# Top-32 attention and a low-rank mixer on one core: another mask for the first batch's heads, a parameter's scaling on GpSimd, and seven buffers for the rounds' maxima

## The chip, the core and the metric

The kernel runs on one core of a Trainium2 chip. A core has a matrix engine (TensorE, PE in the profile), a vector engine (VectorE, DVE), a scalar engine (ScalarE, ACT), a general engine (GpSimd, POOL) and a queue engine (SyncE, SP). Each engine works through its own list of instructions in order, and waits on semaphores where an instruction needs another engine's result. The metric is the time of one execution on the device in microseconds. The kernel before took 1663.71 us in the median of three runs (1663.66 to 1663.92).

## What is computed

Eight batches of eight attention heads, 576 rows each, keep only the 32 largest scores of every row. A mixer with a low-rank matrix over the rows and a two-layer network over the channels follows.

```python
scores = scale * np.matmul(q, k.transpose(0, 1, 3, 2))        # (8, 8, 576, 576), head_dim 64
kth = np.partition(scores, -32, axis=-1)[..., -32:-31]
scores = np.where(scores >= kth, scores, -1e9)
attn = softmax(scores)
x = np.matmul(attn, v) -> (8, 576, 512)
u = x + ((x.T @ U) @ V).T                                      # per batch, rank 32
out = u + np.maximum(u @ w_ch1, 0.0) @ w_ch2                   # 512 -> 2048 -> 512
```

The four parameters of the mixer (U, V, w_ch1, w_ch2) reach the kernel as float64 numbers, that is as pairs of 32-bit words; the kernel turns them into float32 itself.

## The kernel before

**Steps.** Two heads make a pair, so a batch has four pairs (`NPAIR`) and the kernel 32. A step is a tile of 128 rows of a pair, for both heads: t = 0 to 3; the last 64 rows of both heads share one tile, t = 4. In the first batch (pairs 0 to 3) each tile is a step of its own, 20 steps in all (lines 1200 to 1269). In the later batches t = 3 and t = 4 make one step. This document calls the two heads of a step its lanes; lane 1 comes first in every loop, then lane 0.

**The search for the 32 largest.** `front` (line 454) is a generator, advanced piece by piece. In each lane VectorE takes the eight largest of a row (line 507, `first`), strikes them out (line 520, MATCH_VALUE_LOAD and MATCH_REPLACE8) and takes the next eight (line 525), three rounds in all; the eighth value of the last round is the threshold. The rounds' maxima lie in `m8`, allocated anew in each round from a ring of four buffers (line 522). In the first batch the rows are 576 wide; from the second batch on VectorE works on folded rows of 304.

**The masks.** `ways` (line 441) says how each lane is masked once the threshold is known. In the first batch lane 1 of a full tile is "pooled": GpSimd makes the gap (line 530, a comparison and a multiplication by -3e38) and adds it to the scores (line 531), both issued at the end of the step itself. Lane 0, and the one lane of t = 4, take the "gap" way: at the beginning of the next step ScalarE scales the threshold (line 551, `least`), computes the gap with Relu (line 554), and GpSimd subtracts it (line 555). In the later batches both lanes take the "gap" way. The last full tile and the tail of pair 3 have an "early" lane, masked on VectorE. After the mask, `weigh` (line 437) takes the exponential on ScalarE.

**The parameters.** `next_params` (line 218) is called six times per pair in the first batch, besides one call before the loop: after round 1 of t = 0, 1 and 2, and after round 3 of t = 0, 1 and 3. Each call moves three parameters on by a stage: it joins the oldest (`f64_join`: VectorE shifts the bits, line 188; GpSimd adds twice, lines 189 and 191), starts the conversion of the next (`f64_parts`), and loads a third (line 154, on SP's queue, into a ring of three `raw` buffers). The conversion is three ScalarE passes: the scaling (line 176) reads the high words, a second (line 177) rewrites the low words, a third (line 180, Sign) rewrites the high words in place. The passes wait in a list, from which `fill`, called four times a step, takes one each; what is left is issued by the next `next_params`. There are 36 parameters' pieces: 4 of U and V, 16 of w_ch1 and 16 of w_ch2, nearly all 128 x 512 words. A call that finds `len(params)` pieces still unloaded converts piece 35 - `len(params)`.

**Order.** The order on every engine is that of the program (`manual_schedule`); a step of the first batch issues on each engine, in this order: the gap of the step before (lines 551 to 555); the matmuls and the copies of the next step's scores (lines 336, 390 to 392); the values and the transposes of earlier steps (lines 694, 617, 618, 703); `fill`; round 1; `next_params`; `fill`; copies of the next pair's q and k (line 323); round 2; the exponentials of the step before (line 439); `fill`; round 3; `next_params`; the end of the step (lines 530, 531); `fill`.

**The network.** The two layers of a batch are cut into single matmuls, handed out between the steps of the following batch (lines 816 and 834). So the first batch has none of them, and the last batch's come behind the last step (`closing`).

Of the kernel before, what the change touches and what calls it, by code (L numbers as in the profile page):

```python
# [8 lines left out]
F32 = mybir.dt.float32  # L9
U8 = mybir.dt.uint8  # L10
U32 = mybir.dt.uint32
AF = mybir.ActivationFunctionType
ALU = mybir.AluOpType

TOPK = 32
NEG = -3.0e38


RESCALE = 2.0**-112
# [7 lines left out]
def kernel(  # L27
# [28 lines left out]
    nc = tc.nc  # L56
    B, H, S, D = q.shape
    P = 128
# [8 lines left out]
    NPAIR = H // 2  # L67
# [13 lines left out]
    const = ctx.enter_context(tc.tile_pool(name="const", bufs=1))  # L81
    loads = ctx.enter_context(tc.tile_pool(name="loads", bufs=1))
    attn = ctx.enter_context(tc.tile_pool(name="attn", bufs=2))
    small = ctx.enter_context(tc.tile_pool(name="small", bufs=8))
# [37 lines left out]

    nudge = const.tile([P, 1], F32, name="nudge")
    nc.vector.memset(nudge, TINY)
    eps = const.tile([P, 1], F32, name="eps")
    nc.vector.memset(eps, 1e-9)

# [10 lines left out]
        return slice(h * D, (h + 1) * D)  # L138

    SLAB = 512  # L140
    spare = []


# [13 lines left out]
    def f64_parts(raw, out):  # L157

        n, w = raw.shape[0], raw.shape[-1] // 2
        d = "p f" if len(raw.shape) == 3 else "p"
        low, hi = (raw.rearrange(f"{d} (w two) -> {d} w two", two=2)[..., i] for i in range(2))
        low8 = raw.bitcast(U8).rearrange(f"{d} (w eight) -> {d} w eight", eight=8)[..., 3]
        if out is None:
            if not spare:

                uT = mlpp.tile([P, NC, S], F32, tag="uT", name="uT")
                words = uT.rearrange("p c n -> p (c n)").bitcast(U32)  # L170
                spare.extend(words[:, i * SLAB : (i + 1) * SLAB] for i in range(NT))
            out = spare.pop()[0:n, 0:w]
        bits = out.bitcast(U32)
        lows, his = low.bitcast(F32), hi.bitcast(F32)
        passes.extend((
            lambda: nc.scalar.activation(bits.bitcast(F32), his, AF.Copy, scale=RESCALE),
            lambda: nc.scalar.activation(
                lows, low8, AF.Identity, bias=four[0:n], scale=-(1 + 2.0**-10) * 2.0**-26
            ),
            lambda: nc.scalar.activation(his, his, AF.Sign, bias=nudge[0:n]),  # L180
        ))
        return hi, bits, low
# [258 lines left out]
    def ways(g, t):  # L441

        if (g, t) == (NPAIR - 1, NT - 1):
            return (0,), (), (1,)
        if (g, t) == (NPAIR - 1, NT):
            return (0,), (), ()
        if t == NT:
            return (), (), (0,)
        return ((), (1,), (0,)) if g < NPAIR else ((), (), (1, 0))

    def eased(g, t):
        return bool(ways(g, t)[2])

    def front(tiles):

        lanes = []
        for g, t in tiles:  # L460
            if t == 0:
                dens[g] = small.tile([P, 2 * NT + 1], F32, tag="den", name="den", bufs=3)
            S2, den = S2s.pop((g, t)), dens[g]
            early, pooled, gaps = ways(g, t)
            n = S2.shape[1]
            fold_of = folds.pop((g, t), None)
            for c in (1, 0) if n == 2 else (0,):
                slot = c if n == 2 or len(tiles) == 1 else 2
                spot = CH * c + t if g >= NPAIR else 2 * t + c
                lanes.append((  # L470
                    slot,
                    S2[:, c],
                    den[:, spot : spot + 1],
                    [a[:, c] for a in fold_of] if fold_of else None,
                    "early" if c in early else "pooled" if c in pooled else "gap" if c in gaps else "",
                ))
        W = len(lanes)
        first = small.tile([P, 3, 8], F32, tag="first", name="first", bufs=3)
        nmax = small.tile([P, 3], F32, tag="nmax", name="nmax", bufs=4)
        curs, places, ms = {}, {}, {}  # L480
        halves = [(lane[0], *lane[3]) for lane in lanes if lane[3]]
        for at_, step in ((0, 0), (0, 1), (8, 0)):
            for slot, upper, lower in halves:
                spot = upper[:, HALF + at_ : HALF + at_ + 8]
                if step:
                    nc.vector.match_replace(lower, spot, lower, NEG)  # L486
                else:
                    nc.vector.max(spot, lower)  # L488
        for slot, chunk, _, fold_of, _ in lanes:
            if fold_of:  # L490
                curs[slot] = fold_of[0]
            else:
                curs[slot] = chunk
                if slot == 2:
                    places[slot] = attn.tile([P, S], F32, tag="tplace", name="place", bufs=1)
                elif (g, t) == (NPAIR, NT):
                    places[slot] = attn.tile([P, TAIL + S], F32, tag="scale", name="place", bufs=1)[:, 0:S] if slot else (
                        attn.tile([P, NT + 1, P], F32, tag="PTt", name="place", bufs=1)
                    ).rearrange("p c n -> p (c n)")[:, 0:S]
                else:  # L500
                    places[slot] = attn.tile(
                        [P, 2, HALF + TOPK // 2], F32, tag="upper", name="upper"
                    ).rearrange("p c n -> p (c n)")[:, 0:S]
            ms[slot] = first[:, slot]
        order = [lane[0] for lane in lanes]
        for c in order:
            nc.vector.max(ms[c], curs[c])  # L507
        yield
        for i in range(1, TOPK // 8):
            if i == 1:  # L510
                nc.scalar.mul(nmax[:, 0:W], first[:, 0:W, 0], -SCALE)
                Es = {}
                for c, chunk, _, _, way in lanes:
                    if way == "early":
                        Es[c] = attn.tile([P, S], F32, tag="E", name="E")
                        weigh(chunk, Es[c], nmax[:, c : c + 1])
            for c in order:

                nxt = places.pop(c, curs[c])
                nc.vector.match_replace(nxt, ms[c], curs[c], NEG)  # L520
                curs[c] = nxt
            m8 = small.tile([P, 3, 8], F32, tag="m8", name="m8", bufs=4)
            for c in order:
                ms[c] = m8[:, c]
                nc.vector.max(ms[c], curs[c])  # L525
            yield
        for c, chunk, total, _, way in lanes:
            if way == "pooled":
                gap = attn.tile([P, S], F32, tag="E", name="E")
                nc.gpsimd.tensor_scalar(gap, chunk, ms[c][:, 7:8], NEG, ALU.is_lt, ALU.mult)  # L530
                nc.gpsimd.tensor_tensor(chunk, chunk, gap, ALU.add)  # L531
        for c, chunk, total, _, way in lanes:
            if way == "early":
                nc.vector.scalar_tensor_tensor(
                    out=chunk,
                    in0=chunk,
                    scalar=ms[c][:, 7:8],
                    in1=Es[c],
                    op0=ALU.is_ge,
                    op1=ALU.mult,  # L540
                    accum_out=total,
                )
        if t == NT:
            del qkTs[g]
        yield
        gaps = [lane for lane in lanes if lane[4] == "gap"]
        if gaps:
            slots = [lane[0] for lane in gaps]
            lo, hi = min(slots), max(slots) + 1
            least = small.tile([P, 3], F32, tag="least", name="least", bufs=3)  # L550
            nc.scalar.mul(least[:, lo:hi], m8[:, lo:hi, 7], WIDEN)
            for c, chunk, *_ in gaps:
                gap = attn.tile([P, S], F32, tag="E", name="E")
                nc.scalar.activation(gap, chunk, AF.Relu, bias=least[:, c : c + 1], scale=-WIDEN)  # L554
                nc.gpsimd.tensor_tensor(chunk, chunk, gap, ALU.subtract)  # L555
            yield
        rest = [lane for lane in lanes if lane[4] != "early"]
        if len(gaps) > 1:
            c, chunk, total, *_ = rest.pop(0)
            weigh(chunk, chunk, nmax[:, c : c + 1], total)  # L560
            yield
        for c, chunk, total, *_ in rest:
            weigh(chunk, chunk, nmax[:, c : c + 1], total)
        if t == NT and g != NPAIR - 1:
            nc.scalar.activation(den, den, AF.Identity, bias=eps)
        yield
# [615 lines left out]
    t = 0  # L1182
# [177 lines left out]
```

## Time and profile before

| | |
|---|---|
| runs | 1663.92, 1663.71, 1663.66 us |
| profiled execution | 1662.32 us, span of the profile 1660.2 us |
| first batch, 0 to about 205 us | busy: VectorE 194.16, ScalarE 150.62, GpSimd 142.13, TensorE 125.38 us |
| 310 to 1500 us | busy: TensorE 1180.84, VectorE 1186.29 us of 1190 |
| 1500 to 1660 us, the last batch's network | busy: TensorE 153.44, VectorE 67.31 us |
| instructions | 30,248 |

The busy time of each engine, in 40 equal slices of the span, in tenths (9 is 90% or more):

```profile
PE   4566698999899999999999999999999999999999
DVE  7999998999999999999999999999999999994452
ACT  4888778665655666566665666565665656563320
POOL 4787669766656565656656565666666566663620
```

One slice is 41.5 us, so the first five are the first batch.

### The profile page before, as it was taken

What the parts mean: (1) busy time and instruction counts of PE and PEld (TensorE: products, weight loads), DVE (VectorE), ACT (ScalarE), POOL (GpSimd) and SP (SyncE); (2) the same over time, 40 slices, a digit from 0 to 9 for tenths busy, and PEclk for the clock granted to TensorE, in tenths of its full rate; (3) what the DMA queues carried; (4) which work ended last, traced back from release to release, by engine and by line L of the source; (5) the groups of instructions that cost most, each with busy time, mean ns of one, the idle gap of its engine ahead of it and who ended that gap; (6) DMA issues with size and microseconds to landing.
All of it is one profiled execution on the core that took longest, in us unless ns stands there. A gap on an engine that the chain in (4) does not pass through costs nothing.

```text
span 1660.2 us, 30248 instructions
## 1 busy us (share of the span) xinstructions
PE 1555.9 (94%) x9638; PEld 1183.2 (71%) x9638; DVE 1547.4 (93%) x4393; ACT 995.1 (60%) x2475; POOL 1009.4 (61%) x881
## 2 busy tenths in 40 slices
PE   4566698999899999999999999999999999999999
PEld 2444466777677887778777887778777887777776
DVE  7999998999999999999999999999999999994452
ACT  4888778665655666566665666565665656563320
POOL 4787669766656565656656565666666566663620
PEclk7777899999999999999999999999999999999999
DMA  3323223255555555554555565555555555543001
GB/s 88 90 83 92 69 83 86 63 128 133 131 131 130 140 148 138 127 142 130 130 128 137 133 154 133 131 139 133 139 122 142 127 146 135 141 126 97 10 1 29
DMA packets 280399, 189.42 MB, mean 114 GB/s; under 512 B 174288, under 2 KB 261168, under 8 KB 280240
## 3 DMA queue, kind: packets, MB, share of 16 engines
q1 hardware_dynamic: 259728, 117.62, 30.9%
q10 hardware_dynamic: 20512, 69.87, 13.6%
q8 instruction: 76, 1.25, 0.3%
q14 instruction: 83, 0.68, 0.1%
HBM read 116.49 MB, written 70.91 MB: 113 GB/s over the span
## 4 chain that ended last, share of the span: by engine, by line
PE 66%; DVE 25%; DMA 4%; SPq 1%; issue 1%; ACT 1%; POOL 1%; DVEq 0%; ACTq 0%; POOLq 0%
PE mm L834 21%; PE mm L816 19%; DVE m L525 8%; DVE upper L520 7%; PE sc L336 6%; PE O L694 5%; PE mm L910 3%; DVE first L507 3%; PE tp L910 2%; PE sc L910 2%; PE sc L368 2%; DMA PT<-away 2%; PE up L766 1%; DVE y L581 1%; DVE upper L488 1%; DVE place L520 1%
## 5 line engine op out<-in xcount | busy, mean ns | idle before, releaser
L834 PE MATMUL mm<-hT,w 128*128 128x320 f32 (+1 forms) x1792 | 462.1, 407 | 0.0
L816 PE MATMUL mm<-uT,w 128*128 128x320 f32 (+1 forms) x1792 | 459.8, 409 | 1.2 <-ACT hT L829 1.0
L555 POOL TENSOR_TENSOR Ssb<-Ssb,E 128x576 f32<-128x576 f32 x243 | 340.0, 1419 | 185.4 <-ACT E L554 185.2
L816 PEld LDWEIGHTS mm<-uT,w 128*128 128x128 f32 x1792 | 334.1, 190 | 100.7 <-issue 10.6
L834 PEld LDWEIGHTS mm<-hT,w 128*128 128x128 f32 x1792 | 332.0, 190 | 93.0 <-issue 10.2
L525 DVE MAX8 m<-upper 128x8 f32<-128x304 f32 (+1 forms) x774 | 362.5, 509 | 0.7
L520 DVE MATCH_REPLACE8 upper<-m,upper 128x304 f32<-128x304 f32 (+1 forms) x516 | 256.6, 504 | 0.0
L435 POOL TENSOR_TENSOR lower<-lower,upper 128x576 uint32<-128x576 uint32 x108 | 152.5, 1412 | 141.7 <-DVE upper L434 137.2
L432 POOL TENSOR_TENSOR lower<-Ssb 128x576 uint32<-128x576 uint32 x108 | 152.4, 1411 | 116.3 <-ACT Ssb L381 65.9
L439 ACT ACTIVATE Ssb<-Ssb,nmax 128x576 f32<-128x576 f32 x258 | 201.8, 784 | 28.8 <-POOL Ssb L531 10.3
L336 PE MATMUL sc<-qkT 64*128 64x288 f32 (+1 forms) x1056 | 176.9, 457 | 9.1 <-ACT Ssb L390 8.2
L554 ACT ACTIVATE E<-Ssb,least 128x576 f32<-128x576 f32 x243 | 176.3, 769 | 4.2
L488 DVE MAX8 upper<-lower 128x8 f32<-128x288 f32 x432 | 171.8, 438 | 2.3 <-POOL lower L435 2.3
L381 ACT COPY Ssb<-sc 128x576 f32<-128x576 f32 x216 | 127.7, 643 | 66.8 <-PE sc L336 66.3
L829 ACT ACTIVATE hT<-mm 128x320 f32<-128x320 f32 (+1 forms) x224 | 91.9, 411 | 107.3 <-PE mm L816 102.2
L581 DVE STREAM_TRANSPOSE y<-Ssb 128x512 f32<-128x512 f32 (+1 forms) x312 | 153.9, 544 | 0.0
L694 PE MATMUL O<-PT,va 128*64 128x128 f32 x2048 | 144.0, 284 | 0.0
L336 PEld LDWEIGHTS sc<-qkT 64*128 64x128 f32 (+1 forms) x1056 | 95.2, 196 | 49.2 <-issue 17.0
L694 PEld LDWEIGHTS O<-PT,va 128*64 128x64 f32 x2048 | 112.7, 140 | 16.2 <-issue 1.6
L520 DVE MATCH_REPLACE8 upper<-first,upper 128x304 f32<-128x304 f32 x216 | 97.5, 458 | 0.0
L486 DVE MATCH_REPLACE8 lower<-upper,lower 128x288 f32<-128x288 f32 x216 | 93.9, 442 | 0.0
L507 DVE MAX8 first<-upper 128x8 f32<-128x304 f32 x216 | 90.1, 458 | 0.0
(266 smaller groups left out, 2208.4 us busy)
## 6 DMA issues: line engine op xcount, KB each, us to landing
away<-y SPq DMA_DIRECT2D x416, 144.0 KB
PT<-away ACTq DMA_DIRECT2D x104, 576.0 KB
raw<-in_moe_w_ch_dram SPq DMA_DIRECT2D x32, 512.0 KB
va<-in_v_dram SPq DMA_DIRECT2D x64, 128.0 KB
scale<-rd ACTq DMA_DIRECT2D x56, 144.0 KB
out_dram<-ob SPq DMA_DIRECT2D x59, 128.0 KB
ld<-in_q_dram SPq DMA_DIRECT2D x108, 64.0 KB
ld<-in_k_dram SPq DMA_DIRECT2D x108, 64.0 KB
```

The source lines that it names most:

```text
L336: nc.tensor.matmul(out, lhsT=qkT[half(h), 0, cols(t)], rhs=qkT[half(h), 1, lo:hi], start=True, stop=True,)
L435: nc.gpsimd.tensor_tensor(bottom, bottom, top.bitcast(U32), ALU.subtract)
L439: nc.scalar.activation(E, chunk, AF.Exp, bias=nmax, scale=SCALE, accum_out=total)
L488: nc.vector.max(spot, lower)
L520: nc.vector.match_replace(nxt, ms[c], curs[c], NEG)
L525: nc.vector.max(ms[c], curs[c])
L554: nc.scalar.activation(gap, chunk, AF.Relu, bias=least[:, c : c + 1], scale=-WIDEN)
L555: nc.gpsimd.tensor_tensor(chunk, chunk, gap, ALU.subtract)
L581: nc.vector.transpose(y[:, :, i * NT : i * NT + c].rearrange("p r c j -> p c r j"), E2[:, a : a + c * P].rearrange("p (c r j) -> p c r j", ...
L694: nc.tensor.matmul(O[half(h)], lhsT=va[:, h, j, :], rhs=PT[:, NT * h + j], start=False, stop=(j == NT - 1),)
L816: nc.tensor.matmul(ph[:, 0:w], lhsT=first_layer(cc, f), rhs=uT[:, cc, lo:hi], start=(cc == 0), stop=(cc == NC - 1),)
L834: nc.tensor.matmul(po[:, 0:w], lhsT=w2[:, f, c * P : (c + 1) * P], rhs=hTs[f][:, 0:w], start=(f == 0), stop=(f == NF - 1),)
```

## The change

Three things are edited. In the first batch, lane 1 of a full tile takes the "gap" way as lane 0 does; the "pooled" way is gone, and so are its two GpSimd instructions (lines 530 and 531). Both lanes' gaps are then issued at the beginning of the next step, and both exponentials in one piece, as before. The scaling of a parameter's high words (line 176) is done by GpSimd, as a multiplication of two tensors one of which is a column of constants read with a stride of zero, while 12 or more pieces are still unloaded; it is issued at once, right behind the additions of line 191, and not put into the list. And the ring of `m8` has seven buffers. One more memset makes the column of constants.

```diff
+    rescale = const.tile([P, 1], F32, name="rescale")
+    nc.vector.memset(rescale, RESCALE)
...
+    LATE = 12
...
+        if len(params) >= LATE:
+            factor = rescale[0:n] if len(raw.shape) == 2 else rescale[0:n].rearrange("p o -> p o ()")
+            nc.gpsimd.tensor_tensor(
+                bits.bitcast(F32), his, factor.to_broadcast(list(bits.shape)), ALU.mult
+            )
+        else:
+            passes.append(
+                lambda: nc.scalar.activation(bits.bitcast(F32), his, AF.Copy, scale=RESCALE)
+            )
         passes.extend((
-            lambda: nc.scalar.activation(bits.bitcast(F32), his, AF.Copy, scale=RESCALE),
...
     def ways(g, t):
         if (g, t) == (NPAIR - 1, NT - 1):
-            return (0,), (), (1,)
+            return (0,), (1,)
         if (g, t) == (NPAIR - 1, NT):
-            return (0,), (), ()
+            return (0,), ()
         if t == NT:
-            return (), (), (0,)
-        return ((), (1,), (0,)) if g < NPAIR else ((), (), (1, 0))
+            return (), (0,)
+        return (), (1, 0)
...
-            m8 = small.tile([P, 3, 8], F32, tag="m8", name="m8", bufs=4)
+            m8 = small.tile([P, 3, 8], F32, tag="m8", name="m8", bufs=7)
...
-        for c, chunk, total, _, way in lanes:
-            if way == "pooled":
-                gap = attn.tile([P, S], F32, tag="E", name="E")
-                nc.gpsimd.tensor_scalar(gap, chunk, ms[c][:, 7:8], NEG, ALU.is_lt, ALU.mult)
-                nc.gpsimd.tensor_tensor(chunk, chunk, gap, ALU.add)
...
         if len(gaps) > 1:
             c, chunk, total, *_ = rest.pop(0)
             weigh(chunk, chunk, nmax[:, c : c + 1], total)
-            yield
+            if g >= NPAIR:
+                yield
```

More of the change, by code (lines that the diff above doesn't have):

```diff
@@ L443, in ways @@
         if (g, t) == (NPAIR - 1, NT - 1):
-            return (0,), (), (1,)
+            return (0,), (1,)
         if (g, t) == (NPAIR - 1, NT):
-            return (0,), (), ()
+            return (0,), ()
         if t == NT:
-            return (), (), (0,)
-        return ((), (1,), (0,)) if g < NPAIR else ((), (), (1, 0))
+            return (), (0,)
+        return (), (1, 0)
     def eased(g, t):
-        return bool(ways(g, t)[2])
+        return bool(ways(g, t)[1])
     def front(tiles):
@@ L463, in front @@
             S2, den = S2s.pop((g, t)), dens[g]
-            early, pooled, gaps = ways(g, t)
+            early, gaps = ways(g, t)
             n = S2.shape[1]
@@ L474, in front @@
                     [a[:, c] for a in fold_of] if fold_of else None,
-                    "early" if c in early else "pooled" if c in pooled else "gap" if c in gaps else "",
+                    "early" if c in early else "gap" if c in gaps else "",
                 ))
```

## The prediction

> **What bounds the kernel now.** I began with the busy time in stretches: the first batch's second and third pair, then the whole first batch. The columns are the stretch, its length, and the busy time (and instructions) of PE, PEld, DVE, ACT and POOL; TensorE's granted clock, DMA share and GB/s follow.
>
> ```profile
> 57.25:104.00 46.75, 29.23 (x196) 19.50 (x196) 46.48 (x98) 38.68 (x92) 37.95 (x27) 0.78 0.27 78
> 104.00:150.75 46.75, 30.67 (x194) 20.33 (x196) 46.48 (x98) 38.66 (x92) 37.97 (x27) 0.78 0.29 87
> 0.00:205.00 205.00, 125.38 (x781) 83.12 (x781) 194.16 (x411) 150.62 (x362) 142.13 (x116) 0.78 0.30 85
> ```
>
> A pair takes 46.75 us and VectorE is busy for 46.48 of them; both pairs agree to a hundredth, so one pair stands for the next. The waits of VectorE inside those 205 us come next (who waited for whom; us in all, times, longest):
>
> ```profile
> DVE qkT L323 <- PE tp L321: 6.5, 1, 6.5
> DVE Ssb L390 <- PE sc L336: 1.4, 1, 1.4
> DVE first L507 <- ACT Ssb L392: 0.9, 1, 0.9
> ```
>
> All of them belong to the first 12 us. So in the first batch VectorE alone sets the pace; ScalarE and GpSimd, which the change rearranges, have 8 us a pair to spare. It can move the time through VectorE in two ways: by making it wait, or by making an instruction of its own longer. For the second I went to the timeline, at the one VectorE instruction that the edit concerns, the shift of line 188 (start, duration, engine):
>
> ```profile
> 117.07 2.21 POOL L530 TENSOR_SCALAR E<-Ssb,m 128x576 f32<-128x576 f32 x1
> 118.32 0.41 DVE L188 TENSOR_SCALAR w<-w 128x512 uint32<-128x512 uint32 x1
> ...
> 123.48 1.29 POOL L191 TENSOR_TENSOR w<-w,raw 128x512 uint32<-128x512 uint32 x1
> 124.20 0.85 DVE L188 TENSOR_SCALAR w<-w 128x512 uint32<-128x512 uint32 x1
> ...
> 213.55 2.97 POOL L555 TENSOR_TENSOR Ssb<-Ssb,E 128x576 f32<-128x576 f32 x2 [1.87 <-ACT E L554]
> 214.22 1.03 DVE L188 TENSOR_SCALAR w<-w 128x512 uint32<-128x512 uint32 x1
> ```
>
> The shift takes 0.41 us alone, and also inside GpSimd's TENSOR_SCALAR of line 530. Started inside a GpSimd TENSOR_TENSOR it ends only 0.28 us after that one ends (123.48 + 1.29 = 124.77, shift until 125.05; the next VectorE instruction starts 0.2 us after the GpSimd end). At 214.22 it got in between two such instructions. So it loses the remainder of the GpSimd instruction that it meets, and line 530 has been sparing it: six of the shifts of the first batch fall inside line 530 and all take 0.41 us or less.
>
> **The change part by part.** *GpSimd and ScalarE.* Removed are 15 instructions of line 530 and the 15 additions of line 531; the latter return as 15 subtractions of the same size (1408 against 1459 ns). Added are 24 scalings, 21 of them on 512 words. No row shows this multiplication. The nearest is line 739, which also multiplies by an operand read with a stride of zero:
>
> ```profile
> L530 POOL TENSOR_SCALAR E<-Ssb,m 128x576 f32<-128x576 f32 x15 | 33.3, 2222 | 0.0
> L739 POOL TENSOR_TENSOR x<-x,den 128x512 f32<-128x512 f32 x4 | 4.2, 1045 | 6.9 <-ACT x L735 6.9
> L191 POOL TENSOR_TENSOR w<-w,raw 128x512 uint32<-128x512 uint32 x19 | 24.5, 1288 | 1.5
> L554 ACT ACTIVATE E<-Ssb,least 128x576 f32<-128x576 f32 x19 | 14.7, 776 | 0.6
> L176 ACT ACTIVATE w<-raw 128x512 f32<-128x512 f32 x20 | 13.4, 668 | 0.0
> ```
>
> I take its 1.05 us; two whole inputs give 1.29 (line 191), and at worst 512/576 of line 530, 2.0. GpSimd: 21 x 1.05 + 1 - 33.3 = -10 us. ScalarE: 15 x 0.776 - 20 x 0.668 - about 1.3 for the smaller ones = -3 us. Neither bounds the batch, so both count nothing by themselves. If they bounded it, the gain would be 3 us.
>
> *The shifts.* A pair has six, by step and place: A0, B0, A1, B1, A2, B3 (A behind round 1, B behind round 3). Let the shift of a B call start at 0. GpSimd's additions follow at 0.49 and 1.86 and line 530 at 3.12 (145.16, 146.53 and 147.79 after 144.67). In the new order the scaling stands there, until 4.17. Behind it now comes the first subtraction of line 555, because the gaps of the step just ended open the next one; its Relu is done by about 1.1 (round 3 ends, 0.2 for line 551, 0.78 for line 554), so it starts at once, at 4.13, and ends its turn 1.36 later (119.37 to 120.73), at 5.49. The shift of the following A call comes at 4.43 for A1 (113.89 to 118.32) and 4.49 for A2 (124.20 to 129.15, less the 0.46 that the first lost). Both are inside the subtraction, where line 530 was. They can go on at 5.69 in place of 4.75 and 4.81: A1 loses 0.94 us and A2 0.88. With 1.29 for the scaling they lose 1.18 and 1.12.
> B1 gains: it lost 0.46 inside line 191. Now the second subtraction ends at 7.16, the additions at 9.80, the next scaling at 10.85, and the shift comes at 5.69 + 5.56 = 11.25, with GpSimd idle. B0 and B3 find it idle as before. A0 is a close race already: line 555 began at 107.97 and the shift, at 108.01, was not held up; I put 0.1 (0 to 0.2). A pair: 0.1 + 0.94 - 0.46 + 0.88 = 1.46 us, or 2.04 with 1.29.
> The first pair has small pieces. Its A1 lost 0.4 in line 531 and gets that back; its A2, at 35.86, stands behind four additions ending at 35.86, a scaling of 0.32 and a subtraction until 37.55, and goes on at 37.75 in place of 35.95: 1.8 - 0.4 = 1.4 us.
>
> *New waits.* The shift now waits for GpSimd's scaling where it waited for ScalarE's: at A1 the scaling is done 0.26 us before the shift, and with 1.29 only just in time. ScalarE's Sign (line 180) must wait until GpSimd has read the high words: at A1's for 2 to 3 us, by my estimate from these times (the second exponential is done about 2.5 us before that scaling). Behind it in ScalarE's queue stand the gaps, and the copies of the next scores (lines 390 to 392), which VectorE's next `first` needs. In full steps these copies are done 8 us ahead (116.81 against 124.98), at t = 4 some 3.3 us (147.41 against 150.68), less 0.7 for the second Relu; Sign stands behind them there. So I cost this at nothing; without the cover VectorE would idle for what exceeds it. SP's loads (line 154) wait for line 191, which shifts by a microsecond; line 176 never waited for a load in its 20 large instances (0.0 idle), so nothing. The new memset lies in the 6.5 us wait of the start. The seven buffers can give back at most the 0.7 us that line 525 idles in the whole run: nothing.
>
> *The end of the batch.* The last scaling stands ahead of the subtraction of pair 3's last full tile (195.04), whose exponential follows at 196.57 and the copies of the next scores at 197.33 to 198.55; VectorE needs these at 199.18. A microsecond later they end at 199.5: 0.3 us, or 0.55.
>
> *Sum.* 1.4 + 3 x 1.46 + 0.3 = 6.1 us; with 1.29, 1.4 + 6.1 + 0.55 = 8.1. Behind 310 us TensorE and VectorE are both over 99% busy, so what starts later ends later by the same. On the profiled execution (1662.32 us, span 1660.2) that is 1668.4; the runs' median stands 1.4 above it: **1670 us**.
>
> *A rule against it.* The Trainium skill, in "SBUF — State Buffer", "Who interferes with whom", says that GpSimd shares its port pair with a VectorE instruction in a two-port mode, and that whoever issues second is blocked until the first has finished. The TENSOR_TENSOR rows agree; the row of 118.32 inside line 530 doesn't. Were the rule to hold for line 530 too, those shifts would have lost about 1 us already, and the change would come out near nothing.
>
> **The rivals.**
> *No difference.* If the scaling ends so that the shift starts first, or slips between scaling and subtraction, A1 and A2 cost nothing, as A0 did at 108.01, where GpSimd paid (1.72 against 1.41). What is left is -3 x 0.46 and small change: about 1663. For it speaks that the start of the subtraction and the shift lie only 0.3 us apart; against it, that GpSimd needs no signal for its next instruction.
> *More than that.* If the scaling takes 2.0 us, it ends at 5.12, the shift must wait for its result, and the subtraction starts first: VectorE goes on at 6.66 and loses 1.9 at A1 and A2, about 1.2 at A0 and 0.1 at B1, some 5.1 a pair; 1.4 + 15.3 + 1.3 = 18 us, 1682. For it speaks line 530, against it every TENSOR_TENSOR.
> *Faster.* GpSimd, 10 us less busy, could be out of the way of the shifts. Up to 290 us 31 shifts of 512 words take 19.2 us (mean 619 ns) where 31 x 0.41 would take 12.7: if all collisions went, 6.5 us would be won, 1657. It decides from half of that on. But up to 200 us there are only four longer ones, under 2 us in all; the rest lies behind, where nothing changes but the phase.
>
> **How the numbers follow.** A measurement tells about 0.2% (3.3 us) from no change. The forecast, 5 to 11 us slower, has 0.48; more than that 0.15; no difference 0.25; faster 0.12. So slower 0.63, same 0.25, faster 0.12. The range runs from the second case, 1662, to just under 1682, 1680; the likeliest case's own is 1668 to 1675.
>
> **What would show it.** Right: line 188's mean in the first 205 us rises, with A1 and A2 at 1.2 to 1.5 us, each ending 0.3 us after a line 555; a pair takes 48.2 us; the scaling's row is near 1.05 us; VectorE still idles nowhere. Wrong: shifts at 0.41 throughout; waits of VectorE for scores' copies or for the scaling; a pair under 46.75 us.

## The result, and the profile after

The changed kernel takes 1668.8 us in the median of seven runs (1666.81 to 1671.53), the kernel before 1663.71 (1662.5 to 1664.72): the ratio is 1.0032, with a 95% interval from 1.0021 to 1.0043. It is 5.1 us slower. Its profile has a span of 1666.4 us.

The busy times of the changed kernel in stretches show where. The columns are as in the prediction; the first two rows are its second and third pair, each from the subtraction that runs ahead of A0 to the same one of the next pair, the third row is the first 205 us.

```profile
60.26:108.50 48.24, 31.54 (x204) 21.46 (x199) 48.03 (x99) 38.05 (x91) 35.21 (x29) 0.79 0.29 83
108.50:156.72 48.22, 32.28 (x199) 21.99 (x198) 48.01 (x99) 38.02 (x91) 35.22 (x29) 0.75 0.30 87
0.00:205.00 205.00, 125.51 (x743) 84.29 (x743) 194.49 (x400) 146.64 (x347) 130.08 (x124) 0.76 0.30 84
```

A pair takes 48.23 us in place of 46.75, and VectorE is still busy in all but 0.2 us of it, with the same instructions. ScalarE and GpSimd have less to do than before (38.0 and 35.2 us a pair against 38.7 and 38.0), and it doesn't help. So VectorE's own instructions have become longer. The timeline shows which; the shift is now line 199, the scaling line 180, the subtraction line 561 (start, duration, engine).

```profile
118.81 1.04 POOL L180 TENSOR_TENSOR w<-raw,rescale 128x512 f32<-128x512 f32 x1
119.81 2.97 POOL L561 TENSOR_TENSOR Ssb<-Ssb,E 128x576 f32<-128x576 f32 x2
120.09 1.42 DVE L199 TENSOR_SCALAR w<-w 128x512 uint32<-128x512 uint32 x1
...
127.00 0.40 DVE L199 TENSOR_SCALAR w<-w 128x512 uint32<-128x512 uint32 x1
...
131.15 2.96 POOL L561 TENSOR_TENSOR Ssb<-Ssb,E 128x576 f32<-128x576 f32 x2
131.50 1.34 DVE L199 TENSOR_SCALAR w<-w 128x512 uint32<-128x512 uint32 x1
```

The shift of A1 starts 0.28 us after the first of two subtractions, that of A2 0.35 us after, and they take 1.42 and 1.34 us where GpSimd's line 530 once let them pass in 0.41. They end 0.29 us after the first subtraction does: a subtraction takes 1.41 us alone, 119.81 + 1.41 = 121.22, and the shift of A1 ends at 121.51. The pair of subtractions takes 2.97 us, 0.19 more than undisturbed (2.78, at 21.89), as the shift gets in between. B1, at 127.00, is free. The second and the fourth pair have the same numbers (1.43 at 71.85 and 1.34 at 83.26; 1.42 at 168.31 and 1.35 at 179.72).

Other views of the first 205 us of the changed kernel are VectorE's waits, the longest wait of ScalarE, and the rows of the scaling and of the shift; the last line is the shift's row in the kernel before.

```profile
DVE qkT L334 <- PE tp L332: 5.9, 1, 5.9
...
DVE den L636 <- ACT Ssb L450: 0.3, 1, 0.3
DVE uT L199 <- POOL uT L180: 0.2, 1, 0.2
...
ACT raw L191 <- POOL w L180: 18.8, 13, 2.8
...
L180 POOL TENSOR_TENSOR w<-raw,rescale 128x512 f32<-128x512 f32 x20 | 20.9, 1046 | 0.0
...
L199 DVE TENSOR_SCALAR w<-w 128x512 uint32<-128x512 uint32 x19 | 13.6, 714 | 0.0
...
L188 DVE TENSOR_SCALAR w<-w 128x512 uint32<-128x512 uint32 x20 | 10.1, 506 | 0.0
```

The waits of VectorE left out of this list lie in the first 12 us, in both kernels. Only one shift waits for the scaling, for 0.24 us, in the first pair. What stops VectorE is no semaphore: the shift itself has become longer, 714 ns in the mean against 506.

How far the changed kernel lies behind, read off at the same instruction in both traces:

| place | before, us | after, us | difference |
|---|---|---|---|
| first shift | 20.91 | 20.39 | -0.52 |
| B3 of the first pair | 51.15 | 51.51 | +0.36 |
| B3 of the second pair | 97.90 | 99.72 | +1.82 |
| B3 of the third pair | 144.67 | 147.96 | +3.29 |
| B3 of the fourth pair | 191.43 | 196.18 | +4.75 |
| first transpose of q and k on VectorE (line 306, now 317) | 231.07 | 235.96 | +4.89 |
| last maximum on VectorE | 1507.84 | 1512.98 | +5.14 |

Nearly all of it is lost in the first batch, 1.46 us a pair, and is carried to the end. The two profiles' spans differ by 6.2 us, a microsecond more than the last row: behind the last maximum the kernel before takes 152.4 us in its profile and the changed one 153.4. With four buffers in place of seven (below) that stretch takes 151.6, so this microsecond is not put down to the change.

### The profile page after: what moved, and what is told of

It reads as the page before. It is cut to its first block, busy times and chain, and to the rows that moved or that the text cites. A ratio compares the mean times of both kernels' runs of the same rounds, so it can differ in the third digit from the quotient of the medians.

```text
span 1666.4 us, 30224 instructions
## 1 busy us (share of the span) xinstructions
PE 1562.7 (94%) x9638; PEld 1189.9 (71%) x9638; DVE 1552.3 (93%) x4394; ACT 992.9 (60%) x2466; POOL 997.4 (60%) x890
## 3 DMA queue, kind: packets, MB, share of 16 engines
q8 instruction: 76, 1.25, 0.3%
## 4 chain that ended last, share of the span: by engine, by line
DVE 44%; PE 35%; DMA 8%; SPq 5%; ACT 3%; issue 2%; POOL 2%; DVEq 0%; ACTq 0%; POOLq 0%
DVE m L536 11%; DVE upper L531 10%; PE mm L841 10%; PE mm L823 8%; DVE y L588 5%; DVE upper L499 4%; DVE first L518 4%; DVE place L531 3%; PE sc L347 3%; PE mm L917 3%; DMA ld<-in_k_dram 3%; PE O L701 3%; DVE lower L497 2%; DMA ld<-in_q_dram 2%; PE tp L917 2%
## 5 line engine op out<-in xcount | busy, mean ns | idle before, releaser
L561 POOL TENSOR_TENSOR Ssb<-Ssb,E 128x576 f32<-128x576 f32 x258 | 360.6, 1418 | 196.5 <-ACT E L560 196.3
L446 POOL TENSOR_TENSOR lower<-lower,upper 128x576 uint32<-128x576 uint32 x108 | 152.4, 1411 | 146.8 <-DVE upper L445 145.1
L443 POOL TENSOR_TENSOR lower<-Ssb 128x576 uint32<-128x576 uint32 x108 | 152.4, 1411 | 111.4 <-ACT Ssb L392 66.0
L560 ACT ACTIVATE E<-Ssb,least 128x576 f32<-128x576 f32 x258 | 186.3, 768 | 4.2
```

## The experiments

Theory: a shift that meets a GpSimd instruction with two tensor inputs can't use the port it needs until that one ends (in the expectations, the port theory). The traces show that the shift is held up and until when; they show no port. Rivals: the loss comes from having the scaling on GpSimd, because the shift must wait for its result, or because ScalarE's Sign must (it waits 18.8 us in the changed kernel's first batch) and what is queued behind it is late. The kernel before ran again beside the experiments: 1663.03 us (21 runs) beside the first three, 1662.83 us (27 runs) beside the others. The ratios are to these.

**The masks alone.** The changed kernel, with all scalings on ScalarE.

```diff
-    LATE = 12
+    LATE = 100
```

> The changed kernel with all scalings on ScalarE again, so the masks and the seven buffers alone. Port theory (a shift that meets a GpSimd instruction with two tensor inputs waits for its end): behind a B call the first subtraction now follows the additions directly, from 3.12 to 4.5 us, and the shifts of A1 and A2 at 4.43 and 4.49 fall on its end: 0 to 0.3 us each, or 1.3 where the second subtraction starts first; B1 is free (-0.46). A pair takes 46.3 to 47 us, the whole 1662 to 1666. Rival (the shift, or ScalarE's Sign, waits for GpSimd's scaling): nothing is left to wait for, 1663.7, a pair 46.75 us or less.

Measured: 1660.68 us (11 runs), ratio to the kernel before 0.9985, interval 0.9977 to 0.9994. A pair takes 46.27 us. Its timeline, GpSimd's subtractions and the shifts of A1, B1 and A2:

```profile
115.40 2.97 POOL L561 TENSOR_TENSOR Ssb<-Ssb,E 128x576 f32<-128x576 f32 x2
116.67 0.42 DVE L199 TENSOR_SCALAR w<-w 128x512 uint32<-128x512 uint32 x1
122.58 0.40 DVE L199 TENSOR_SCALAR w<-w 128x512 uint32<-128x512 uint32 x1
...
125.72 3.04 POOL L561 TENSOR_TENSOR Ssb<-Ssb,E 128x576 f32<-128x576 f32 x2
127.08 0.40 DVE L199 TENSOR_SCALAR w<-w 128x512 uint32<-128x512 uint32 x1
```

Without the scaling in front, the first subtraction starts a microsecond earlier against the shift. A1 (1.27 us after its start) and A2 (1.36 us after) meet its very end, lose nothing, and the second subtraction waits in their place. So the masks by themselves are a gain of 2.4 us. That is less time than either side expected (1662 to 1666 by the port theory, which had allowed for some loss at A1 and A2, and 1663.7 by the rivals), and it doesn't tell them apart. Some 1.9 us of the gain are what shifts had lost before inside a two-input instruction: B1 (0.84 to 0.41 us) in three pairs, and 0.66 us at the A1 of the first.

**The scaling alone.** The kernel before, with the scaling moved to GpSimd as in the change; the pooled masks stay.

```diff
+        if len(params) >= LATE:
...
+            nc.gpsimd.tensor_tensor(
+                bits.bitcast(F32), his, factor.to_broadcast(list(bits.shape)), ALU.mult
+            )
...
         passes.extend((
-            lambda: nc.scalar.activation(bits.bitcast(F32), his, AF.Copy, scale=RESCALE),
```

> The kernel before with only the scaling moved to GpSimd; the pooled masks stay. GpSimd then has the scaling at 3.12 to 4.17 us behind a B call and line 530 from 4.13. Port theory: the shifts of A1 and A2 at 4.43 and 4.49 fall 0.3 us after the start of line 530, an instruction with one tensor input, and take 0.41 us (no shift of the kernel before fell so early into it; if it holds the port at first, they take up to 2.2). But GpSimd, 6 us a pair busier than before, reaches the scaling that B1 needs only at about 12.8 us where the shift comes at 10.3: B1 waits some 2.4 us. A pair about 48.5 us, the whole 1670 to 1672. Rival (the loss of the change comes from waiting for the scaling, not from the port): about the same time, so the time alone does not tell them apart; the lengths of the shifts do.

Measured: 1672.68 us (5 runs), ratio 1.0061 (1.0047 to 1.0075); the second and third pair take 49.99 and 49.37 us. The timeline (line 541 is the former line 530):

```profile
121.34 1.05 POOL L180 TENSOR_TENSOR w<-raw,rescale 128x512 f32<-128x512 f32 x1
122.36 2.21 POOL L541 TENSOR_SCALAR E<-Ssb,m 128x576 f32<-128x576 f32 x1
122.42 0.96 DVE L199 TENSOR_SCALAR w<-w 128x512 uint32<-128x512 uint32 x1
...
131.06 0.43 DVE L199 TENSOR_SCALAR w<-w 128x512 uint32<-128x512 uint32 x1 [2.12 <-POOL w L180]
...
135.53 2.47 POOL L541 TENSOR_SCALAR E<-Ssb,m 128x576 f32<-128x576 f32 x1
135.58 0.43 DVE L199 TENSOR_SCALAR w<-w 128x512 uint32<-128x512 uint32 x1
```

Here the rival is right for this kernel, as both sides expected: B1 waits for the scaling, 2.11, 2.12 and 2.93 us in the three pairs, because GpSimd, at 43.7 us a pair, is late. It is not what the change suffers from, which took that load off GpSimd again: there one shift waits, for 0.24 us. The half of the expectation on the A shifts failed, and the time is a little above the 1670 to 1672 expected. Three of six take 0.96 us in place of 0.41, so the instruction with one tensor input does hold the shift up, but only for a part of its time: the shift begun at 122.42 ends at 123.38, which by estimate lets the shift go on 0.74 us after line 541's start, if 0.28 us of it remain behind the release, as after a TENSOR_TENSOR. Where the shift got ahead (135.58), GpSimd's instruction grew to 2.47 us.

**The scaling first.** The changed kernel with the scaling issued ahead of the two additions of the same call; the same instructions on every engine.

```diff
-        while parts:
-            f64_join(*parts.pop(0))
+        older = parts[:]
+        parts.clear()
         while raws:
...
+        for part in older:
+            f64_join(*part)
```

> The changed kernel with the scaling issued ahead of the two additions of the same call, not behind them; GpSimd has the same instructions. Port theory: the subtraction behind a B call starts at 3.12 in place of 4.13 us, and the shifts of A1 and A2 meet its last tenth: 0.1 to 0.3 us each in place of 0.94 and 0.88; B1 may meet a scaling (0.5 us). A pair about 46.9 us in place of 48.2, the whole 1664 to 1665. Rival (ScalarE's Sign waits for GpSimd, 19 us in the first batch, and what is behind it comes late): Sign still waits wherever GpSimd is behind, so most of the loss stays, 1667 or more.

Measured: 1663.41 us (11 runs), ratio 1.0002 (0.9993 to 1.0011). The third pair in the busy times, then GpSimd and the shifts of A1 and B1 in it:

```profile
107.42:154.08 46.66, 31.94 (x193) 22.02 (x192) 46.45 (x99) 37.23 (x90) 34.84 (x29) 0.71 0.30 88
...
116.54 2.98 POOL L563 TENSOR_TENSOR Ssb<-Ssb,E 128x576 f32<-128x576 f32 x2
117.82 0.42 DVE L199 TENSOR_SCALAR w<-w 128x512 uint32<-128x512 uint32 x1
...
123.11 1.03 POOL L180 TENSOR_TENSOR w<-raw,rescale 128x512 f32<-128x512 f32 x1
123.72 0.70 DVE L199 TENSOR_SCALAR w<-w 128x512 uint32<-128x512 uint32 x1
```

The changed kernel's whole loss is gone with one instruction of GpSimd's list moved past two others. The subtractions lie where the masks alone had them, and A1 and A2 pass in 0.42 and 0.41 us. B1 meets a scaling now and loses 0.3 us. The time is a little under the 1664 to 1665 that the port theory expected, and far from the rival's 1667 or more. The work is the same, on the same engines, so the load of GpSimd or the scaling's place on it can't by itself explain the loss. Against the masks alone 2.7 us remain. Shifts that now meet a scaling lose 2.3 us: 0.3 us at B1 of three pairs, 0.72 once in the first pair (24.66, 0.88 us), and 0.07, 0.07 and 0.53 at the three A0 (60.77, 107.42, 154.08).

This run doesn't settle the rival of the Sign by itself. Its expectation, that Sign would still wait wherever GpSimd is behind, was wrong: in the first 205 us of this kernel Sign waits for GpSimd not once, where it waited 18.8 us in the changed kernel. So the two went away together. Two other things rule that rival out. In the changed kernel ScalarE's lateness would have to reach VectorE as a wait, and VectorE has none in the full pairs. And the next run makes the loss without any scaling on GpSimd.

**Two inputs in place of one.** The kernel before, with nothing on GpSimd but line 530 changed.

```diff
-                nc.gpsimd.tensor_scalar(gap, chunk, ms[c][:, 7:8], NEG, ALU.is_lt, ALU.mult)
+                nc.gpsimd.tensor_tensor(gap, chunk, ms[c][:, 7:8].to_broadcast([P, S]), ALU.mult)
```

> The kernel before with line 530 turned from an instruction with one tensor input (2.22 us) into a multiplication with two, the second a column read with a stride of zero (about 1.2 us); it leaves out the comparison, so lane 1 of the first batch is not masked. GpSimd has 15 us less to do, nothing else moves. Port theory: the shifts of A1 and A2 now meet line 531, from about 4.25 us, and lose about 1 us each; A2 of the first pair loses 1.3; B1 gains 0.46. A pair 48 to 48.5 us, the whole 1668 to 1671, slower with less work. Rival (the loss of the change comes from having the scaling on GpSimd): 1663.7 or a little less.

Measured: 1666.4 us (11 runs), ratio 1.0022 (1.0013 to 1.0031): slower, with 15 x (2.22 - 1.15) = 16 us less to do on GpSimd and no scaling there. A pair takes 47.65 us. A1 and A2 in the timeline:

```profile
119.47 1.73 POOL L531 TENSOR_TENSOR Ssb<-Ssb,E 128x576 f32<-128x576 f32 x1
119.53 0.41 DVE L188 TENSOR_SCALAR w<-w 128x512 uint32<-128x512 uint32 x1
...
129.78 1.41 POOL L531 TENSOR_TENSOR Ssb<-Ssb,E 128x576 f32<-128x576 f32 x1
129.91 1.57 DVE L188 TENSOR_SCALAR w<-w 128x512 uint32<-128x512 uint32 x1
```

The rivals said no loss. The rows account for the 0.9 us a pair: 0.16 lost at A0 (109.06, 0.56 us), 1.16 at A2, and 0.44 won at B1. The size is half of what the port theory said, and the rows above show why: A2 came 0.13 us after line 531 had begun and lost 1.2 us; A1 came 0.06 us after its recorded start and won, and GpSimd's instruction took 1.73 us in place of 1.41.

**Four buffers.** The changed kernel with `bufs=4` for `m8`.

> The changed kernel with four buffers for the rounds' maxima, as before. Theory: the buffers do nothing, as VectorE never waits for one: 1667 to 1670, the lengths of the shifts unchanged. Rival (the buffers carry part of the result): another time by more than 2 us, with waits of VectorE at line 536.

Measured: 1668.67 us (6 runs) against 1668.8 for the change. The buffers do nothing.

**More of the conversion in the first batch.** The masks alone, with a further call of `next_params` per pair behind round 3 of t = 2, and then a second one behind round 1 of t = 3.

```diff
-            if t in (0, 1, NT - 1):
+            if t < NT:
                 next_params(1)
```

> The masks alone (1660.7) with one more call per pair in the first batch, behind round 3 of t = 2. Four to five shifts move out of the stretch from 200 to 310 us, where they take 1.0 to 1.4 us, into places where GpSimd is idle or at the end of an instruction, 0.32 us each. Port theory: 3 us less, 1657 to 1659, if VectorE bounds the stretch behind the first batch; a pair 46.6 us. Rival (TensorE bounds that stretch, or ScalarE, at 43.4 of 46.6 us a pair, becomes late with the copies of the scores): 1661 to 1664.

> As f1, with a second further call per pair, behind round 1 of t = 3: eight calls a pair, eight to nine shifts moved. Port theory: 5 us less than the masks alone, 1655 to 1657, a pair 46.9 us. Rival: ScalarE, at about 45.5 of 46.9 us a pair, delivers the scores' copies late and VectorE waits: a pair 47.5 us or more, 1661 to 1666.

Measured: 1661.92 and 1662.01 us (11 runs each), ratios 0.9991 (0.9982 to 1.0000) and 0.9993 (0.9984 to 1.0002); neither beats the masks alone. The port theory's 1657 to 1659 and 1655 to 1657 failed; the rivals' ranges hold. In the first the shifts moved much as expected: a pair takes 46.85 us, no shift lies behind 266 us where the masks alone have four, and the 512-word shifts take 15.8 us in all against 19.1. But VectorE's waits between 205 and 310 us, first of the masks alone and then of this kernel, tell where most of the gain went:

```profile
DVE upright L641 <- ACT den L572: 2.2, 1, 2.2
DVE w L199 <- ACT w L185: 1.9, 2, 1.7
DVE upper L499 <- POOL lower L446: 1.3, 1, 1.3
...
DVE upright L641 <- ACT den L572: 4.0, 2, 2.2
DVE upper L499 <- POOL lower L446: 3.7, 2, 2.7
...
```

The waits grow from 5.4 to 8.1 us, two of 0.2 us that aren't shown included: most of the 3.3 us won at the shifts comes back as waits for GpSimd's folding (line 446) and ScalarE's denominators (line 572). Why these are late isn't settled, and the rest isn't accounted for. With the second call two shifts of each of the last three pairs are longer again (about 0.66 us behind round 3 of t = 2, 0.94 behind round 1 of t = 3), and in the last pair two more (1.59 us at A0, 0.78 at B3). Its first transpose on VectorE stands at 235.57 us against 228.43, with eight more shifts done by then.

## Why the prediction was right

The forecast was 1670 us, from a sum of +6.1 us; measured is +5.1.

*What bounds.* VectorE sets the pace of the first batch in both kernels, and what ScalarE and GpSimd were relieved of counted nothing, as costed: they had 10 and 13 us a pair to spare in the end.

*The scaling's price.* Taken from line 739 at 1.05 us; its own row says 1.046.

*The shifts.* A pair was to lose 1.46 us; the three full ones lost 1.46, 1.47 and 1.46. A1 and A2 were to start inside the first subtraction, 0.30 and 0.36 us after its beginning; they start 0.28 and 0.35 us after. B1 gained what was expected. A0 lost nothing where 0.1 was put (109.76, 0.43 us), and A1 and A2 lost 1.01 and 0.93 us in place of 0.94 and 0.88. So the mechanism came out place by place; that the sum agrees to a hundredth is luck, as these differences cancel. The scaling first and two inputs in place of one show the mechanism by itself, once by removing it and once by making it. They show too how fine the forecast was: with the subtraction a microsecond earlier under the shift the loss is gone, and the start that decided it was worked out to 0.02 us.

*The first pair.* Predicted 1.4 us, measured 0.88 (from -0.52 to +0.36): its A1 gained 0.66 in place of 0.4, and its A2 took 1.39 us and waited 0.24, a little less than the 1.8. The start of the kernel, before any changed instruction on VectorE, lay 0.52 us earlier in this profile; the same place stands between 20.30 and 20.90 us in the experiments, so that is no effect of the change. Counted from the first shift to the last maximum the profile has lost 5.66 us where the sum has 6.1, which is the first pair's 0.5 us less 0.1 behind it. The medians' 5.1 us can't be taken apart as finely: the start alone varies by 0.6 us from profile to profile.

*The end of the batch.* Predicted 0.3 us of waiting for the scores' copies. VectorE waits 0.27 us there, but one instruction earlier, at line 636, for the sum of the late exponential (line 450): the size was right, the instruction was not, so the agreement is luck. Nor had the sum anything for the shifts that come next. In the kernel before, those at 203.53 and 214.22 took 1.12 and 1.03 us; their places in the changed one take 0.41 (208.70, 218.68), and one that took 0.43 (225.16) takes 1.24 (229.24). With the short waits these nearly cancel: the lag grows by 0.14 us from the last B3 to the first transpose.

*New waits.* ScalarE's Sign does wait for GpSimd, 18.8 us in all and at most 2.8, and it costs nothing, as the copies of the scores still come in time. Seven buffers: nothing, as expected.

*Where it was wrong.* The reading that line 530 spares the shift "also inside" it holds only for the part where the shifts of the kernel before fell, 1.25 us and more after its start. The scaling alone put shifts at its beginning, and there it holds them up. For the change this made no difference, as line 530 is gone from it.

*The skill's rule.* The Trainium skill, in "SBUF — State Buffer", "Who interferes with whom", has the second to issue wait for the whole of the first, where the VectorE instruction is in a two-port mode. Starts that lie within 0.07 us of each other aside, nothing here contradicts that for GpSimd's TENSOR_TENSOR (1.42, 1.34, 1.57 us). For its TENSOR_SCALAR the measurement differs: 0.96 us at the beginning, 0.41 us later on, within a span of 2.2 us.

## What to carry to other kernels

Before work is moved to an engine that has room, look at what will run on it at the moments when the bound engine issues an instruction that it can hold up: here 1 us more in front of an instruction of GpSimd cost 0.9 to 1.0 us at each of two VectorE instructions a pair, though GpSimd as a whole had become less busy. Such losses don't show as waits, only as longer instructions; the spread of one line's durations (0.40 to 1.43 us) is the view to look at. And a change of several parts is worth taking apart: the masks alone gain 2.4 us on the kernel before, and the scaling costs 9.6 alone and 8.1 on top of the masks.

## What the runs showed of the hardware

- A GpSimd TENSOR_SCALAR with a span of 2.2 us held up VectorE's shift for its first 0.74 us or so, by estimate (0.96 us for a shift begun 0.06 us after the start), and let one begun 1.25 us or more after it pass (0.41 us). No shift here starts in between.
- When both engines come within 0.07 us, either can win. With GpSimd's recorded start 0.04 to 0.07 us ahead, a 512-word shift of the second to fourth pair won six times of six against a TENSOR_TENSOR (three in the kernel before, three with two inputs; 0.40 or 0.41 us, GpSimd's instruction 0.31 to 0.33 us longer) and three times of six against the TENSOR_SCALAR of the scaling alone (0.43 us, GpSimd's instruction 0.25 to 0.27 us longer); the other three took 0.96 us. At 0.12 to 0.14 us behind a TENSOR_TENSOR's start it lost, three times of three (1.56 to 1.58 us).
- Of two GpSimd instructions back to back, a shift that waits for the first gets in ahead of the second (2.97 us for the two in place of 2.78).
